# Attention and rational MLP on one core: quad 1's loads moved from the software queue to the two hardware issuers, products of zeros ahead of the first transposes, and a re-searched static plan

One core of a Trainium2 chip. The metric is device time of one execution in microseconds (us); most executions agree within 0.3%. "g1" is the product with w_in throughout, and "the start" is the time of its first matmul.

## The reference

```python
# ... cut: m is each row's maximum, h2 = h * h, h3 = h2 * h ...
scores = scale * np.matmul(q, k.transpose(0, 1, 3, 2))      # q, k, v: 8 x 12 x 448 x 64, float32
e = np.exp(scores - m)
attn = e / (np.sum(e, axis=-1, keepdims=True) + np.exp(-m) + 1e-09)
x = np.matmul(attn, v)      # then heads joined: 3584 x 768
h = x @ w_in                # 768 x 2048
P = a[0] + a[1] * h + a[2] * h2 + a[3] * h3
Q = 1.0 + np.abs(b[0]) * np.abs(h) + np.abs(b[1]) * h2
out = (P / (Q + 1e-06)) @ w_out                              # 2048 x 768
```

## The kernel before

Every instruction is an `Op` with an engine, an estimated duration and dependencies. A small simulation in the kernel file (`Plan`) merges several lists for each engine into one order, and the kernel emits that order. Changing a constant of the plan therefore reorders instructions without changing any of them.

Batch 0 is attended in half-width "units" (queries 0 to 223 of the four-head "quads" 0, 1, 2, ...), so that g1 can begin early. For quad 0, pieces of k and q come as float32 to staging tiles, are cast to float16, transposed on PE, copied from PSUM, multiplied to scores on PE and exponentiated on ScalarE:

```python
piece(0, 0, 0, 2, "ACT", 2.8, "ACT")     # k, pair 0, first half: issued by ACT, cast by ACT
piece(1, 0, 0, 2, "SP", 2.65, "DVE")     # q
piece(0, 0, 2, 2, "ACT", 3.4, "ACT")
piece(1, 1, 0, 2, "SP", 3.9, "DVE")
piece(0, 1, 0, 2, "ACT", 3.6, "ACT")
piece(0, 1, 2, 2, "SP", 3.7, "ACT")
for pr in range(2):
    piece(1, pr, 2, 2, "SP", 6.8, "DVE", True)      # late: waits for a stage
# ... cut ...
kload.append(load_op(1, k, kn, "k", kfree, NN))     # quad 1 by the software queue (POOL)
qload.append(load_op(1, q, qn, "q", qfree, NN))
loads(0, "v")
loads(2, "kq")
loads(1, "v")
loads(2, "v")
ORDER = "kq3 i kq4 i kq5 v3 i v4 i v5 o kq6 o o o"  # i, o: pieces of w_in, w_out
```

One unit's attention is 48 matmuls (16 for the sums of the exponentials, 32 with v), then a logarithm and an exponential on ScalarE that make the reciprocal:

```python
ln = Op(f"ln{i}", "ACT", 0.14 + 0.4 * f, [], None)
ex = Op(f"ex{i}", "ACT", 0.14 + 0.35 * f, [ln], None)
d = Op(f"a{i}d", "PE", 0.77 * f, [consts, hist(x_free, b, NX)] + e_ops[m0:m0 + 2 * npass],
       lambda: tiles(ud, lambda h, j: ones[0:P, :]), gen=(True, ud, ln), mode="a")
```

## Time and profile before

| | before |
|---|---|
| time, median of 3 | 432.91 us (432.63 to 433.24) |
| span of the profiled execution | 431.5 us |
| start (first g1 matmul) | 27.30 us |
| from the start to the end | 404.21 us, of it 1.35 us of PE stalls and 3.33 us after the last matmul |
| first exponential | 8.19 us |
| record of full TensorE clock begins | 18.08 us |

The time is the span and some 1.8 us around it. PE is close to solid behind the start, so a gain must come from an earlier start, from fewer stalls behind it, or from the tail. ScalarE paces the stretch ahead of it (15.49 us of work in the 19.18 from the first exponential on). In its order of time (columns: start, duration, instruction, and in brackets the idle time just before it with what ended it) the waits of the old stretch are:

```profile
10.22 1.92 ACT L480 ACTIVATE e<-sps 112x896 f16<-112x896 f32 x2 [0.32 <-PE sps L472]
12.78 1.72 ACT L480 ACTIVATE e<-sps 112x896 f16<-112x896 f32 x2 [0.64 <-PE sps L472]
14.92 0.45 ACT L521 ACTIVATE lden<-gen,one_c 128x224 f32<-128x224 f32 x1 [0.42 <-PE gen L507]
16.89 1.72 ACT L480 ACTIVATE e<-sps 112x896 f16<-112x896 f32 x2 [1.10 <-PE sps L472]
19.65 0.92 ACT L480 ACTIVATE e<-sps 112x896 f16<-112x896 f32 x1 [1.04 <-PE sps L472]
```

All of them end with a score pass or an attention group on PE: ScalarE waits for PE, and PE, at that time, runs slowly (16 attention matmuls take 0.94 us at 13.93 and 0.57 at 19.73) or waits for a load (k of quad 3, issued at 10.01 us, is waited for until 18.88).

### The profile page before, as it was taken

The numbers are of one execution on the slowest core, as the hardware profiler recorded it, in microseconds if no ns is written. First come the engines' busy times: TensorE is split into PE (matmuls) and PEld (weight loads), VectorE is DVE, ScalarE is ACT, GpSimd is POOL, SyncE is SP. The second block draws the span as 40 slices with busy tenths as digits, with TensorE's granted clock in tenths as the row PEclk, the third lists the DMA queues.
The fourth block names the chain that finished last, engine by engine and source line by source line (L and its number), as shares of the span: only waits on it lengthen the run. The fifth ranks groups of instructions, "written<-read, shape, count | busy, mean of one in ns | idle before, by whom it ended". The sixth has DMA issues, their size and how long they took to land.

```text
span 431.5 us, 8834 instructions
## 1 busy us (share of the span) xinstructions
PE 419.2 (97%) x3680; PEld 218.7 (51%) x3680; DVE 339.9 (79%) x505; ACT 327.8 (76%) x386; POOL 120.7 (28%) x172
## 2 busy tenths in 40 slices
PE   3999999999999999999999999999999999999996
PEld 2667665544444444444454444444444455555563
DVE  2445999998999887698998668979698788999800
ACT  4699999798888777888886897877798854578521
POOL 5655516566005340423703333052000000000000
PEclk9999999999999999999999999999999999999999
DMA  9999999899606947299399886373211011111132
GB/s 148 202 200 205 207 180 150 152 154 162 123 2 69 160 85 118 28 141 115 58 117 107 119 123 85 81 108 73 45 36 38 2 36 38 36 38 36 39 103 81
DMA packets 78153, 43.12 MB, mean 100 GB/s; under 512 B 36128, under 2 KB 74528, under 8 KB 78112
## 3 DMA queue, kind: packets, MB, share of 16 engines
q0 software_dynamic: 37856, 22.35, 39.7%
q1 hardware_dynamic: 39472, 19.80, 25.5%
q8 instruction: 29, 0.48, 0.5%
q10 hardware_dynamic: 784, 0.39, 0.4%
q14 instruction: 12, 0.10, 0.1%
HBM read 45.62 MB, written 11.01 MB: 131 GB/s over the span
## 4 chain that ended last, share of the span: by engine, by line
PE 89%; ACT 4%; DMA 3%; DVE 1%; issue 1%; ACTq 0%; POOLq 0%
PE gen L671 34%; PE gen L573 33%; PE gen L507 12%; PE sps L472 10%; DMA kn<-in_k_dram 2%; ACT e L480 2%; DMA h<-in_k_dram 1%; ACT c L625 1%; ACT c L628 1%; PE gen L389 1%; DVE h L590 0%; ACT lden L521 0%; DVE x L535 0%; ACT lden L523 0%; DVE c L614 0%
## 5 line engine op out<-in xcount | busy, mean ns | idle before, releaser
L480 ACT ACTIVATE e<-sps 112x896 f16<-112x896 f32 x192 | 167.1, 917 | 41.5 <-PE sps L472 41.1
L573 PE MATMUL gen<-x,w_in 128*128 128x448 f16 (+1 forms) x864 | 161.8, 332 | 0.0
L671 PE MATMUL gen<-w_out,g 128*128 128x384 f16 (+2 forms) x768 | 135.9, 326 | 0.0
L573 PEld LDWEIGHTS <-w_in 128*128 128x128 f16 x864 | 79.9, 98 | 68.3 <-issue 14.4
L671 PEld LDWEIGHTS <-g 128*128 128x128 f16 x768 | 72.7, 98 | 58.4 <-issue 10.4
L590 DVE CAST h<-gen 128x448 f16<-128x448 f32 x113 | 69.4, 618 | 24.4 <-PE gen L573 24.3
L614 DVE TENSOR_TENSOR n<-n,h 128x1792 f16<-128x1792 f16 x64 | 70.1, 1095 | 0.7
L625 ACT ACTIVATE c<-c,oneeps_c 128x1792 f16<-128x1792 f16 x32 | 57.3, 1791 | 11.4 <-DVE c L614 11.1
L472 PE MATMUL sps<-qt,kt 64*128 64x448 f16 (+1 forms) x432 | 58.4, 343 | 2.3 <-ACT e L480 1.1
L648 POOL COPY gx<-g 128x1024 f16<-128x1024 f16 x8 | 8.3, 1040 | 183.1 <-DVE g L614 183.1
L693 ACT ACTIVATE o<-gen 128x384 f32<-128x384 f32 (+2 forms) x56 | 27.4, 490 | 36.2 <-PE gen L671 36.0
L628 ACT ACTIVATE c<-c 128x1792 f16<-128x1792 f16 x32 | 54.6, 1705 | 0.3
L610 DVE TENSOR_SCALAR n<-n,abc 128x1792 f16<-128x1792 f16 x64 | 44.3, 693 | 1.1
L614 DVE TENSOR_TENSOR g<-n,c 128x1792 f16<-128x1792 f16 x32 | 35.1, 1098 | 12.8 <-ACT c L628 11.5
L433 POOL COPY kp<-kn 112x256 uint32<-112x256 uint32 x36 | 26.1, 755 | 57.2 <-DMA kt<-kp 50.3
L507 PE MATMUL gen<-e,vn 112*32 112x448 f16 (+1 forms) x864 | 41.8, 337 | 0.0
L535 DVE TENSOR_TENSOR x<-gen,lden 128x448 f16<-128x448 f32 (+1 forms) x54 | 28.3, 563 | 13.9 <-ACT lden L523 12.7
L614 DVE TENSOR_TENSOR c<-c,w 128x1792 f16<-128x1792 f16 x32 | 35.2, 1100 | 0.0
L472 PEld LDWEIGHTS <-kt 64*128 64x128 f16 x432 | 15.0, 96 | 36.5 <-issue 32.9
L507 PEld LDWEIGHTS <-vn 112*32 112x32 f16 x864 | 23.1, 99 | 14.0
L433 POOL COPY qp<-qn 112x256 uint32<-112x256 uint32 x36 | 25.2, 726 | 18.1 <-DMA qt<-qp 18.0
L610 DVE TENSOR_SCALAR n<-h,abc 128x1792 f16<-128x1792 f16 x32 | 24.7, 772 | 0.1
(42 smaller groups left out, 248.1 us busy)
## 6 DMA issues: line engine op xcount, KB each, us to landing
vn<-in_v_dram POOLq DMA_DIRECT2D x24, 224.0 KB, 8.5
kn<-in_k_dram POOLq DMA_DIRECT2D x23, 224.0 KB, 5.7
qn<-in_q_dram POOLq DMA_DIRECT2D x23, 224.0 KB, 7.4
w_in<-in_moe_w_in_dram POOLq DMA_DIRECT2D x12, 256.0 KB, 9.7
w_out<-in_moe_w_out_dram POOLq DMA_DIRECT2D x4, 768.0 KB, 16.2
out_dram<-o SPq DMA_DIRECT2D x8, 336.0 KB, 3.2
out_dram<-o SPq DMA_DIRECT2D x8, 288.0 KB, 2.8
out_dram<-o SPq DMA_DIRECT2D x7, 240.0 KB, 2.5
```

The costliest lines, as they stand in the source:

```text
L433: nc.gpsimd.tensor_copy(out=mid[0].bitcast(U32)[:, pr], in_=src[n % NN].bitcast(U32)[:, 2 * pr:2 * pr + 2] .rearrange("p e j d -> p j e d"))
L472: nc.tensor.matmul(out=sps[m % NS][0:(P if i == 0 and j == 1 else 128), hh, ci * qw:(ci + 1) * qw], lhsT=kt[n % NK][r, c0:c0 + (P if i == ...
L480: nc.scalar.activation(out=e_sb[m % NE], in_=sps[m % NS][0:P, :, 0:S], func=AF.Exp, scale=scale)
L507: nc.tensor.matmul(out=gen[unit["bank"]][32 * h:32 * h + 32, 0:qw], lhsT=lhs(h, j), rhs=e_sb[m % NE][:, h % 2, c0:c0 + qw], start=(j == 0) ...
L535: mult.emit = lambda s=s, uu=uu: nc.vector.tensor_tensor(out=x_sb[b % NX][:, 2 * qd + s, q0:q0 + qw], in0=gen[uu["bank"]][:, 0:qw], in1=ld ...
L573: nc.tensor.matmul(out=gen[unit["bank"]][:, fi * qw:(fi + 1) * qw], lhsT=w_in_sb[wg][:, c // 2, c % 2, (fc % FG) * 128:(fc % FG + 1) * 128 ...
L590: nc.vector.tensor_copy(out=dst, in_=src)
L610: return lambda: nc.vector.tensor_scalar(out=out, in0=in0, scalar1=s1, scalar2=s2, op0=op0, **kw)
L614: return lambda: nc.vector.tensor_tensor(out=out, in0=in0, in1=in1, op=ALU.mult)
L625: lambda: nc.scalar.activation(out=c, in_=c, func=AF.Ln, bias=oneeps_c)))
L628: lambda: nc.scalar.activation(out=c, in_=c, func=AF.Exp, scale=-1.0)))
L671: nc.tensor.matmul(out=gen[unit["bank"]][:, 0:wd], lhsT=lhs, rhs=w_out_sb[f][:, fc % FG, cols], start=(fc == 0), stop=(fc == NFC - 1))
```

## The change

The intent: let the clock of TensorE rise before the real work comes, by multiplying zeros while PE has nothing to do (that work raises it was the author's assumption; what the runs show of it stands below); give the pieces of quad 0 the DMA engines alone, and let quad 1 come by the two hardware issuers; and let the plan be searched again with a model of how loads share the DMA engines. The core of the diff:

```diff
+    def fill(n, out):
+        for _ in range(n):
+            nc.tensor.matmul(out=out[0:64, 0:P], lhsT=idle[0:P, 0:64], rhs=idle[0:P, :],
+                             start=True, stop=True)
+    FIRST = 32                    # zeros ahead of the first transposes
+    FILLS = (4, 4, 3, 1)          # ahead of score passes 0 to 3
     def scores ... emit:
+                    if m < len(FILLS):
+                        fill(FILLS[m], sps[m % NS][:, 0])
-        piece(0, 0, 0, 2, "ACT", 2.8, "ACT")
+        plan.add("c0", piece(0, 0, 0, 2, "ACT", 2.8))           # cast on DVE now
+        plan.add("c0", piece(0, 0, 2, 2, "ACT", 3.0, "ACT"))    # the one cast left to ACT
 ...
+            for ti, (src, dst, dma) in enumerate(((k, kn, "ACT"), (q, qn, "SP"))):
+                stage = quad1_stage(ti, pr)
+                d = load(dma, src, 4 + 2 * pr, 2, stage, 0, J, 4.3 + 1.1 * pr)
+                cast(1, ti, pr, 0, J, dst[1][:, 2 * pr:2 * pr + 2], stage, d)
 ...
-    kload.append(load_op(1, k, kn, "k", kfree, NN))
-    qload.append(load_op(1, q, qn, "q", qfree, NN))
+    vz = plan.add("cpt", Op("vz", "DVE", 0.06, [first_casts[0, 1, 0, 0]],
+                            lambda: nc.vector.memset(vn[0][:, 0, 0, 0:2], 0.0)))
     loads(0, "v")
+    vload[0].deps.append(vz)      # v of quad 0 held behind the first q cast
-    ORDER = "kq3 i kq4 i kq5 v3 i v4 i v5 o kq6 o o o"
+    ORDER = "kikiikivkkvoovoovkvv"
-    DUES = (0, 0, 4, 6)
-    LEAD = 45.0
+    DUES = (0, 0, 4.2, 3.0)
+    LEAD = 50.9
+    DUE = (28.1, 39.7, 51.4, 58.5, 76.4, ... cut ...)
-    TLEAD = 5.0
+    TLEAD = 4.6
-    LAG = {0: L0, 1: L1, B - 2: L6, B - 1: (8, 2)}
+    LAG = ((0, 3.5), (12.0, 1.8), (6.5, 2.4), (5.0, 1.9), (4.0, 3.4), (12.0, 1.8), (11.5, 2.8), (12.0, 1.3))
```

Cut: the new model of transfers, and bookkeeping that lets output tiles be planned in another order.

> **What bounds the kernel now.** I read the page first, then the busy time in stretches, the chain that ended last, the timelines of TensorE and ScalarE up to 30 us, and the DMA issues with their landings.
>
> ```profile
> PE 419.2 (97%) x3680; PEld 218.7 (51%) x3680; DVE 339.9 (79%) x505; ACT 327.8 (76%) x386; POOL 120.7 (28%) x172
> PE   3999999999999999999999999999999999999996
> DMA  9999999899606947299399886373211011111132
> ```
>
> TensorE is full from the second slice on. A busy PE is not a PE at its peak, so I split the trace at the first matmul of the first product with w_in (27.3 us; line L573, "g1" below):
>
> ```profile
> 0.00:8.19 8.19, 1.63 (x20) 1.01 (x20) 2.19 (x20) 2.74 (x5) 5.68 (x13) 1.00 0.76 135
> 8.19:27.37 19.18, 17.25 (x341) 11.46 (x340) 8.41 (x28) 15.49 (x23) 10.58 (x15) 1.00 1.36 200
> 27.37:67.30 39.93, 39.92 (x557) 26.99 (x558) 31.52 (x55) 37.88 (x47) 16.36 (x24) 1.00 1.30 197
> 67.30:399.58 332.28, 331.81 (x2595) 162.24 (x2592) 288.73 (x394) 262.40 (x299) 87.00 (x120) 1.00 0.58 84
> ```
>
> The first columns are stretch, length, PE busy. From 27.4 us PE has next to no idle time. There I took the gaps from matmul start to matmul start: g1 189 ns for 448 columns, the product with w_out 163 ns for 384, and each change of kind costs the same every time (0.19 us out of a score pass, 0.10 us into one from a product, 0.24 us out of an attention group). Gaps beyond these sum to about 1.3 us in 404 us. So behind g1 the kernel is a fixed amount of PE work, and only its start can be moved. Ahead of g1 the matmuls need about 11 to 13 us by those gaps, but 27.3 us pass: some 15 us are lost there, 4.0 of them before the first matmul.
>
> How they are lost, on ScalarE and PE:
>
> ```profile
> 7.56 0.72 ACT L351 ACTIVATE kn<-h 112x256 f16<-112x256 f32 x2 [2.74 <-DMA h<-in_k_dram]
> 8.19 1.70 ACT L480 ACTIVATE e<-sps 112x896 f16<-112x896 f32 x2
> ...
> 13.93 0.94 PE L507 MATMUL gen<-e,ones 112*32 112x224 f16 x16
> 17.15 0.59 PE L389 MATMUL gen<-ident,kn 112*64 112x112 f16 x8
> 18.93 0.39 PE L389 MATMUL gen<-ident,kn 112*64 112x112 f16 x8 [0.37 <-DMA kn<-in_k_dram]
> 19.73 0.57 PE L507 MATMUL gen<-e,ones 112*32 112x224 f16 x16
> ```
>
> ScalarE stands 2.74 us at a cast that waits for a piece of k; the first exponential, whose scores were ready at 5.5 us, starts at 8.19. And the same 16 matmuls take 0.94 us at 13.93 and 0.57 us at 19.73: PE runs cold. The trace's clock record for full speed begins at 18.08 us (the PEclk row does not show this). The chain says the rest:
>
> ```profile
> 1.72 5.82 DMA h<-in_k_dram
> 10.01 8.87 DMA kn<-in_k_dram
> ```
>
> Early pieces land late because the software queue was already filled behind them, and the k load of quad 3 is waited for at 18.88, ahead of unit 2's scores.
>
> [...]full speed is recorded from 18.08 to 431.10 us, which is 121.0 windows; the window 14.67 to 18.08 was full of work, the one before had a gap at 11.7 to 12.2. [...]a 112 KB piece issued at 0.74 us lands after 2.5 us, one issued at 8.00 into the backlog after 6.4.
>
> **The change part by part.**
>
> *Products of zeros.* 32 of 112 columns ahead of the first transposes, 4, 4, 3 and 1 ahead of the first score passes. [...] They need only a memset that ends near 0.9 us, so they run from about 1.1 to 4.1 us, in time in which PE idles (first transpose at 3.99). The cost is about 0.1 us there, and 12 x about 50 ns = 0.6 us later, most of it while PE waits for copies; I count 0.3 us. The gain: with the window grid of the trace (18.08 minus multiples of 3.413: 1.02, 4.43, 7.84) PE is warm at 4.4 or 7.8 us instead of 18.1. PE was busy without a gap from 12.2 to 18.1 us; at full clock (0.57 against 0.94, 0.39 against 0.59: ratio 0.6 to 0.66) these 5.9 us shrink to about 3.7.
>
> *First loads.* Quad 1's k and q come by four 224 KB loads (f32 in SBUF) on SP and ACT; the software queue starts with v of quad 0, held by a memset behind the first q cast (about 4.4 us). So the six first pieces have the DMA alone: at the 240 KB per us that the packets of 2 to 4 us show, 672 KB from 1.9 us are through at about 4.7 (before: 7.54), the 896 KB of quad 1 at about 8 (before: 8.87 and 10.08).
>
> *Casts.* Three of ScalarE's four k casts move to VectorE; the one left waits for a piece that landed at 4.38. The first exponential then starts behind its scores, about 5.4 us instead of 8.19: 2.8 us. VectorE gains three k casts and four casts of 512 columns, some 3 us, in a stretch in which it is busy 8.4 of 19.2 us; but they stand in front of copies and wait for landings, so the fourth exponential is held to about 9 us.
>
> *Order of loads.* Behind v0: k2, q2, v1, v2, k3, q3, w_in 0, k4, q4, w_in 1 and 2, k5, q5, w_in 3. One load of 224 KB lands per 1.15 us in a backlog, a w_in piece per 1.3. From about 9 us on: k2 10.5, q2 11.6, k3 15 to 16 (before 18.88), w_in 0 at 20 to 21 (before 23.45), w_in 3 near 36 (42.62). PE's order wants w_in 3 some 17 us behind g1: no wait.
>
> *The new plan behind g1.* In PE's order of both programs the matmuls behind g1 are the same (864 and 896 of the two products, 1152 of attention, 364 of scores) but 16 more transposes (0.4 us). Changes into and out of score passes are 102 and 102 before, 101 and 101 after. With the measured costs: 393.3 us before, 393.0 after. So 0.3 us gained.
>
> **The sum.** When does g1 start? ScalarE decides: until the reciprocal of unit 2 it has 14 exponentials at 0.80 us (start to start) and three pairs of 0.34 and 0.28: 13.1 us. Before, it took 17.95 us from 8.19 to 26.14, so 4.9 us were waits, and g1 came 1.2 us later. After: 5.4 + 13.1 + 1.2 = 19.7 us with no wait. A warm PE and earlier k3 take part of the 4.9; the held fourth exponential and quad 2's landing keep some. I choose 3 us: g1 at 22.7, 4.6 us earlier. With 0.3 of the plan gained, 0.3 for the zeros inside and 0.3 for new stalls: 432.9 - 4.6 - 0.3 + 0.3 + 0.3 = 428.6; the chance that some of the old 1.3 us of stalls goes brings me to 428.3.
>
> **Rivals.**
> 1. *The zeros don't warm it*, or the window grid falls otherwise and the sparse work after 4 us doesn't hold it. The cold loss stays in part; the loads and casts alone give about 2.5 us: 430.4. For it: 4 to 12 us had some half of the time in work and stayed cold. Against: the three runs agree to 0.6 us.
> 2. *ScalarE becomes the bound later.* The new plan draws attention forward: unit 16 starts 141 us behind g1 instead of 160. Summing start-to-start times in ScalarE's order, work up to unit 16's last exponential exceeds PE's position there by 5.4 us; at units 3 to 5 it is 13.8 in both programs, so 8 us of slack are left against the start. VectorE: 3.7 at unit 15 against 14.5 at unit 0. But waits between the engines in the denser plan could cost 1 to 3 us: 430 to 431.
> 3. *DMA only moves the wait.* The engines are full until about 50 us; the f32 staging writes twice the bytes of a cast load. If quad 2 lands 2 us later than I say, g1 starts near 24.5: 430.2.
> 4. *Everything fits*: g1 near 20 us, 425.6.
>
> **Range and chances.** 2% is 8.7 us; even g1 at its floor of 19.7 and all old stalls gone give 7.6 + 1.3 + 0.3 = 9.2 us, so faster by over 2% needs everything at once. Slower by over 2% needs over 13 us of new stalls behind g1, which neither engine's sums show. Eight in ten: 425.6 (rival 4) to 431.0 (rivals 1 and 2 in part).
>
> **What would show it.** Clock record at full from 4.4 or 7.8 us; 16 attention matmuls at 0.57 us from the first group on; first exponential at 5.3 to 5.7 us, no long ScalarE wait at a cast; first matmul with w_in at 22 to 23.5 us; PE idle behind it under 2 us and score changes as counted. Wrong if PE stays cold beyond 8 us, if g1 comes at 25 us or later, or if g1 is early but PE waits for ScalarE or VectorE between 100 and 170 us.

Where cuts are marked, statements about the hardware that no trace of this case shows are taken out, among them the working-out of the zeros' length (3.0 us), from which "about 1.1 to 4.1 us" comes. The changed kernel's trace has the 32 zeros from 0.98 us to the first transpose at 3.98, so 94 ns each; at full clock ten of them took 0.48 us (8.03 to 8.51, second profile with zeros in the waits). No term of the sum itself is cut: it came to 428.6 us, and to 428.3 with fewer stalls. But its 3 us of waits rest on a PE that is warm at 4.4 or 7.8 us, and that on the author's assumption that a "window" of 3.413 us full of work raises the clock. The grid of these windows is borne out by the records below, the assumption only in part.

## The result

The changed kernel took 431.74 us (median of 430.96, 431.62, 431.92, 431.85), the kernel before 432.77 (432.91, 432.63, 433.24, 432.04). All runs are in the fast state. Ratio 0.9974, 95% interval 0.9955 to 0.9993; in a later call with more rounds 0.9965 (0.9950 to 0.9981). Ratios here are the mean time of one kernel's fast runs over that of the other's in the same rounds, so not quite the ratio of the medians. The change gains 1 to 1.5 us where 4.6 were predicted: "within 2%" holds, the range 425.6 to 431.0 doesn't.

From the changed kernel's page, the shares of the engines and the row of TensorE's clock (before, that row shows 9 in all 40 slices):

```profile
PE 421.0 (98%) x3724; PEld 222.1 (52%) x3724; DVE 340.1 (79%) x514; ACT 328.1 (76%) x383; POOL 112.3 (26%) x170
PEclk8799999999999999999999999999999999999999
```

The 44 more matmuls are the zeros. A changed kernel that looks colder than the one before is an artefact: the record of before begins only at 18.08 us, with the full clock, and its row shows 9 ahead of that too, although 16 attention matmuls take 0.94 us there (at 13.93), as long as in the changed kernel at a recorded clock of 0.50 (at 12.44). The changed kernel's record reads: full from 4.88 to 8.30 us, half to 15.12, full to 428.14. These stretches are 1, 2 and 121 times 3.413 us long, and the full one of before 121 times; a window, below, is one such 3.41 us, counted from the steps of its profile. **The clock rose as early as predicted and fell again one window later.** Busy time by these windows (columns: stretch, length, PE busy and matmuls, granted clock, DMA share, GB/s; the 1.00 ahead of the first step, at 4.88 us, is the same artefact, as the zeros there take 94 ns each):

```profile
1.47:4.88 3.41, 3.41 (x42) 1.00 0.80 212
4.88:8.30 3.42, 2.29 (x36) 1.00 1.08 264
8.30:11.71 3.41, 2.65 (x33) 0.50 1.44 197
11.71:15.12 3.41, 3.41 (x68) 0.50 1.41 202
```

The zeros and the first eight transposes fill the first window entirely. In the next one PE has 2.29 us of work in 3.42, and behind it the clock is at 0.50. ScalarE in the changed kernel, in its order of time:

```profile
5.59 0.90 ACT L540 ACTIVATE e<-sps 112x896 f16<-112x896 f32 x1
6.81 0.92 ACT L540 ACTIVATE e<-sps 112x896 f16<-112x896 f32 x1 [0.32 <-PE sps L532]
7.94 0.92 ACT L540 ACTIVATE e<-sps 112x896 f16<-112x896 f32 x1 [0.22 <-PE sps L532]
10.09 2.53 ACT L540 ACTIVATE e<-sps 112x896 f16<-112x896 f32 x3 [1.23 <-PE sps L532]
13.43 0.45 ACT L581 ACTIVATE lden<-gen,one_c 128x224 f32<-128x224 f32 x1 [0.80 <-PE gen L567]
15.35 2.58 ACT L540 ACTIVATE e<-sps 112x896 f16<-112x896 f32 x3 [1.05 <-PE sps L532]
```

The first exponential comes at 5.59 us instead of 8.19: that gain is there. Then the waits: 1.23, 0.80 and 1.05 us are the large ones. I count waits as the prediction did, from the first exponential to the first one behind unit 2's reciprocal, less 13.1 us of work: 4.7 us before (8.19 to 26.03; the prediction's 4.9 took 26.14 from the chain) and 4.9 after (5.59 to 23.58). None of it has gone. What stands behind the last two waits is PE at half clock (0.50 by the record; at full clock the same 16 and 32 matmuls take 0.57 and 0.94 us, fourth profile below), as its order of time shows:

```profile
12.44 0.94 PE L567 MATMUL gen<-e,ones 112*32 112x224 f16 x16
13.16 1.71 PE L567 MATMUL gen<-e,vn 112*32 112x224 f16 x32
```

and what stands behind the 1.23 us is a load. The chain of waits (start, duration, what) goes from the landing of quad 1's k to the score pass that unit 0 waits for, though that pass uses no data of quad 1: the cast and the transposes of quad 1 stand ahead of it in the orders of VectorE and PE.

```profile
2.23 5.56 DMA g<-in_k_dram
...
7.81 0.67 DVE kn L375
...
8.52 0.96 PE gen L446 x16
...
9.56 0.51 PE sps L532 x4
...
10.09 0.93 ACT e L540
```

So the start comes at 24.85 us, 2.45 earlier than in the first profile of before. Behind it, 404.31 us against 404.21: PE stalls 1.00 against 1.35 us (gaps from matmul start to matmul start beyond what the same change of kind costs elsewhere), but 3.75 against 3.33 us after the last matmul.

### The profile page after: what moved, and what is told of

Read it like the earlier page. It is cut to its first block, busy times and chain, and to the rows that moved or that the text cites. A ratio compares the mean times of both kernels' runs of the same rounds, so it can differ in the third digit from the quotient of the medians.

```text
span 429.2 us, 8939 instructions
## 1 busy us (share of the span) xinstructions
PE 421.0 (98%) x3724; PEld 222.1 (52%) x3724; DVE 340.1 (79%) x514; ACT 328.1 (76%) x383; POOL 112.3 (26%) x170
## 4 chain that ended last, share of the span: by engine, by line
PE 90%; DVE 5%; ACT 2%; DMA 1%; ACTq 0%; issue 0%
PE gen L731 35%; PE gen L633 33%; PE gen L567 12%; PE sps L532 10%; ACT e L540 2%; DMA g<-in_k_dram 1%; DVE n L670 1%; DVE n L674 1%; DVE h L650 1%; DVE c L674 0%; PE gen L446 0%; DVE c L670 0%; ACTq L370 0%; DVE qt L454 0%; DVE kt L454 0%; DVE w L670 0%
## 5 line engine op out<-in xcount | busy, mean ns | idle before, releaser
L532 PE MATMUL sps<-qt,kt 64*128 64x448 f16 (+1 forms) x432 | 57.3, 338 | 2.0 <-ACT e L540 1.3
L708 POOL COPY gx<-g 128x1024 f16<-128x1024 f16 x8 | 9.4, 1173 | 155.0 <-DVE g L674 155.0
L491 POOL COPY kp<-kn 112x256 uint32<-112x256 uint32 x36 | 23.0, 667 | 42.7 <-DMA kt<-kp 38.8
L329 POOL DMA_DIRECT2D vn<-in_v_dram x24 | 17.5, 732 | 57.5 <-PE sps L532 43.9
```

The lines of the kernel that those rows point to most:

```text
L532: nc.tensor.matmul(out=sps[m % NS][0:(P if i == 0 and j == 1 else 128), hh, ci * qw:(ci + 1) * qw], lhsT=kt[n % NK][r, c0:c0 + (P if i == ...
```

## Experiments

Sixteen runs, all correct. Single looks (the last four) have state "unknown"; every other one has its profile from an execution in the fast state, and of all their executions one is slow (438.12 us, with both orders and the zeros).

### Are the zeros worth anything by themselves?

Without zeros:

```diff
-    FIRST = 32
-    FILLS = (4, 4, 3, 1)
+    FIRST = 0
+    FILLS = (0, 0, 0, 0)
```

> The changed kernel without its 44 products of zeros, all else equal. Theory A (the zeros warm TensorE for one window only, 4.9 to 8.3 us, and the clock drops again to 15.1 us because too little work follows): without them the clock record starts at 11.7 to 18.1 us, once, and stays; the first matmul with w_in comes 0.3 to 1.0 us later than the changed kernel's 24.85, so about 0.5 us slower than the changed kernel, 1.5 to 2 us faster than the kernel before in the profiled span. Rival B (the clock at the start is not on the path, loads and casts decide): within 0.2 us of the changed kernel. Rival C (the zeros cost more than they give): 0.3 us or more faster than the changed kernel.

431.39 us, 0.9968 (0.9953 to 0.9984): the same as with them. The profiled execution has its first exponential at 5.63, full clock from 15.27 us only, and the start at 25.10. The kernel before with the 44 zeros:

```diff
+        nc.vector.memset(idle, 0.0)
+    FIRST = 32
+    FILLS = (4, 4, 3, 1)      # and the two calls of fill() as in the change
```

> The kernel before with the same 44 products of zeros and nothing else. Theory A: warm for one window at most, then cold again, since the kernel before has still less work between 4.4 and 7.8 us (it waits for the pieces of k until 7.5): 0 to 0.7 us faster than the kernel before. Rival B: 0. Rival D (a clock that is held makes the dense stretch 12.2 to 18.1 us shorter by 2.2 us): 2 us faster, which needs the clock at full from 8 us on.

432.85 us, 1.0003 (0.9983 to 1.0023); in its profile the clock is full from 17.51 us and the start is at 27.44. Products of zeros in this number are neutral in either kernel. The early first exponential is the work of loads and casts alone.

### Can the clock be held, and what is that worth?

84 more zeros, ahead of score passes and transposes up to pass 11:

```diff
-    FILLS = (4, 4, 3, 1)
+    FILLS = (4, 8, 8, 2, 6, 6, 8, 8, 4, 4, 4, 4)
+    TFILLS = {2: 6, 4: 4, 8: 12, 10: 8}       # zeros ahead of these transposes
```

> The changed kernel with 84 more products of zeros, spread over the first 12 score passes and four groups of transposes, most where TensorE waits[...]. Theory A (the clock's drop at 8.30 us and the cold stretch to 15.12 us cost about 2 us): the clock record has no gap after its first start, the 16 attention matmuls of unit 0 take 0.57 us and not 0.94, first matmul with w_in at 22.7 to 23.5 us, total 1.3 to 2.0 us below the changed kernel. Rival B (ScalarE waits for landings and for VectorE's casts, whatever the clock): clock held, but the first matmul with w_in stays at 24.5 to 25, same time within 0.3 us. Rival C: the zeros stand in TensorE's order ahead of what is wanted, and eat the gain.

432.13 us, 0.9984 (0.9969 to 0.9999). The clock is full from 6.93 us without a gap, yet the start is at 25.84. The chain says why (shares of the chain up to 27 us): the zeros themselves are its largest part.

```profile
by line: PE sps L272 26.0%; PE sps L536 17.2%; PE gen L450 12.5%; PE gen L571 10.1%; ACT e L544 9.5%; PE gen L272 7.3%; issue 4.9%; PE gen L637 2.5%; DVE x L599 2.2%; ACT lden L585 1.6%; DVE kt L458 1.5%; ACT lden L587 1.0%; DVE qt L458 0.7
```

So I put 29 more zeros only where PE had been waiting:

```diff
-    FILLS = (4, 4, 3, 1)
+    FILLS = (4, 4, 4, 1)
+    TFILLS = {2: 4, 4: 4, 8: 12}
+    PRE = {5: (10, 8)}                         # 8 ahead of score pass 5
```

> The changed kernel with 29 more products of zeros, put only where TensorE waits in its trace: 4 ahead of the transposes at 5.7 and 6.7 us, 12 ahead of quad 1's (7.9 to 8.5 us), 8 into a free bank ahead of score pass 5 (10.5 to 11.0), one more ahead of pass 2. Theory A' (a held clock is worth some 1.5 us, which the zeros on TensorE's path ate in the run with 84 more): clock at full without a gap from its first start, exponential 6 at 13.8 to 14.3 us and not 15.35, first w_in matmul at 23.5 to 24, 1 us faster than the changed kernel. Rival E (the clock moves ScalarE's waits only from one place to another, because landings of k and q follow): first w_in matmul 24.5 to 25.5, same time as without any zeros (431.4) within 0.4 us.

430.48 us, 0.9958 (0.9941 to 0.9976). In the profile the clock is full from 10.72 us; the start is at 24.48. Repeated beside the changed kernel on one chip:

> The changed kernel with 29 more products of zeros where TensorE waits, once more, now beside the changed kernel on the same chip. If holding the clock is worth about 1 us without the zeros standing on the path, ratio 0.995 to 0.996 to the kernel before and 0.5 to 1.2 us under the changed kernel. If the ratio of 0.9958 was the luck of its chip, it comes out at 0.997 to 0.998, level with the changed kernel. In the profile: full clock from before 11 us without a gap, attention group of unit 0 at about 1.0 us of matmul spacing instead of 2.3.

430.27 us, 0.9954 (0.9934 to 0.9974), against 431.18 us, 0.9965 (0.9950 to 0.9981), of the changed kernel. It is the best version that I ran and beats the kernel before by 0.4 to 0.5%; against the changed kernel the intervals overlap, so that part (0.9 us of medians) isn't established. In this profile the clock is full from 4.38 us and stays, and the start is at 23.35.

### Is it the order of quad 1's work?

No zeros, and quad 1's casts and transposes behind unit 0's last score pass:

```diff
-            more = {-1: first[:2], 0: first[2:3], 1: first[3:], 2: nxt[:2]}
+            more = {-1: first[:2], 0: first[2:3], 1: first[3:], 3: nxt[:2]}
```

> No zeros; quad 1's casts on VectorE and transposes on TensorE put behind what unit 0's last score pass needs. Theory F (the fourth exponential waits 1.3 to 1.9 us for quad 1's landing and casts though it uses no data of quad 1): exponential 3 at 9.2 us or earlier instead of 10.1 to 10.5, and the first w_in matmul 0.3 to 0.8 us earlier than in the run without zeros (25.10), as the fifth exponential still needs quad 1. Rival E: the wait only moves to exponential 4, nothing gained.

430.85 us, 0.9965 (0.9949 to 0.9980), no better than without zeros alone. The fourth exponential comes at 9.43 instead of 10.47, the fifth, which does need quad 1, at 10.92 and the seventh at 14.90. The start (26.84) can't be compared here, as the plan put one more attention group ahead of it. With unit 0's attention moved behind unit 1's third score pass as well:

```diff
-            if t == 1:
+            if t == (2 if i == 1 else 1):
```

> As the run before it, and unit 0's attention group (48 matmuls, 2.4 us on a cold TensorE) behind unit 1's third score pass. Theory G (ScalarE's longest wait, between exponentials 5 and 6, is TensorE's order: score pass 6 stands behind the cold attention group): exponential 6 at 13.2 to 13.8 us, first w_in matmul 1 to 1.5 us earlier than without zeros. Rival: the reciprocal of unit 0 comes later by what is gained, and the end stays.

433.26 us, 1.0024 (1.0004 to 1.0044). The seventh exponential comes at 13.27, the eighth then only at 16.13: the wait moved by one pass. And both together with the zeros in the waits:

> Both changes of order, and the zeros in the waits. Theory A' with F and G: the effects add in part: first w_in matmul at 22.5 to 23.5 us, 1.5 to 2 us faster than the changed kernel, 429.7 to 430.2. Rival E: 431 or more.

432.51 us, 1.0014 (0.9978 to 1.0050; two of six executions are far out: 436.74, which counts as fast and is in the ratio, and 438.12, which is slow and is not; no run explains them). Here the clock is full from 5.15 us and the start is at 24.03, but 406.76 us follow it, 2.66 of them stalls. The two other orders of quad 1's work gain no time. They pass waits on, within the stretch or to what comes behind the start.

### The plan or the start?

The changed kernel with the plan's old constants:

```diff
-    DUES = (0, 0, 4.2, 3.0)
+    DUES = (0, 0, 4, 6)          # LEAD, due times, TLEAD and LAG of before too
```

> The changed kernel with the due times, lead and lags of the kernel before (the search's results behind the first w_in matmul undone; loads, casts and zeros kept). If the new plan behind that matmul is neutral, as the two traces say (404.2 us behind it before, 404.3 after): same time as the changed kernel within 0.5 us. If the old constants don't fit the earlier start: new waits of TensorE behind it, 0.5 to 2 us slower than the changed kernel.

432.32 us, 0.9996 (0.9979 to 1.0013), start at 25.89. The other half, the new constants on the first loads and casts of before, without zeros:

```diff
-        plan.add("c0", piece(0, 0, 0, 2, "ACT", 2.8))
+        piece(0, 0, 0, 2, "ACT", 2.8, "ACT")      # and so on: loads and casts of before
```

> The first loads and casts of the kernel before, no zeros, but the changed constants of the plan. If the plan is what gains, ratio 0.997 to 0.998, with g1 at 27 us and the stretch behind it at 403 to 404 us. If the earlier first pieces and the plan are only worth something together (the old plan on the new start gave 0.9996), ratio 1.000, with g1 at 26 to 27.5 us and 404.3 us or more behind it. A plan that was searched for another start may also lose: then 1.001 to 1.004.

432.96 us, 1.0007 (0.9986 to 1.0028), start at 26.36. Neither half gains anything measurable; together they gain 0.3%. (The interval of the old plan and that of the changed kernel, 0.9950 to 0.9981, overlap slightly, so what the new plan adds to the new loads isn't established.) This run also dates the tail: 3.33 us after the last matmul, as before, while the old plan on the new loads has 3.75. The longer tail goes with the loads: in all profiles it is 3.33 to 3.43 us with the loads of before and 3.60 to 3.77 with the new ones.

### How far do two profiles of one kernel differ?

> The kernel before, unchanged, as a kernel of its own: shows how far two sets of runs of the same instructions differ, and gives a second profile. All theories expect a ratio of 1.000 with an interval of at most 0.002 to each side. Should it miss 1 by 0.002 or more, differences of that size among the other runs (0.9968 without zeros, 0.9958 with zeros in the waits) tell nothing. In its profile g1 at 27.1 to 27.5 us, 404.2 to 404.6 us behind it, and the clock's full step first seen between 15 and 18.5 us.

Ratio 1.0002 (0.9988 to 1.0017), as expected of the same instructions. But its profile has the start at 25.98, not 27.1 to 27.5, and 405.18 us behind it with 2.23 us of stalls: the page that the prediction rests on shows a late start of this kernel. Its clock was full from 14.87 us instead of 18.08.

> The changed kernel, unchanged: the common reference of this call, and a second profile. Expected ratio 0.997 (0.9974 in the first result), span 429.2 to 430.2. My theory says that the early full clock comes and goes again, because the second window has too little work: full by about 5 to 7 us, half again before 12 us, full for good at 14 to 18 us. The rival, that the drop in the first profile was a chance of the phase, expects a clock that stays full from 5 us in this one.

Here both theories missed. The clock never rose early: it is full from 16.38 us on. The zeros, 0.98 to 4.1 us, fell on both sides of a boundary at 2.73 us (counted back from that step), and the windows behind it had 3.17, 3.17 and 2.87 us of work; the clock was full only behind the next, with 3.41. Every execution lists its mean granted clock, and this says how often the other case comes, as cold time ahead of the first step doesn't count there (1.000 in the first profile of before, full from 18.08 us) and a clock that is lost again does: 0.988 to 0.992 in six of the changed kernel's twelve executions (the first profile, with two windows lost, has 0.991), and never below 0.998 without zeros or in the kernel before. A rise with a drop behind it is thus common, and it is worth nothing that shows: in this call the three executions at 0.991 have a mean of 430.96 us, the other three 431.56, and the ranges (430.51 to 431.38, 430.93 to 432.26) overlap.

(The 0.37 in the third of the next expectations stands in no view: that window was 67% busy, 2.29 us of 3.42.) What was left open was whether the clock or the landings set the start. Four more looks, two of each version:

> The version with 29 more zeros in the waits, only for a third profile of it. Its two profiles have the clock full from 10.72 us with the first w_in matmul at 24.48, and full from 4.38 us with it at 23.35: 0.18 us per us of half clock. If the clock sets the start, this profile lies within 0.35 us of 23.35 + 0.18 x (start of full clock - 4.38), with ScalarE's waits growing in step. If that was chance, the start has nothing to do with the clock record.

> The same once more: within 0.35 us of 23.35 + 0.18 x (start of full clock - 4.38), if the clock sets the start.

> The changed kernel for a third profile. Its two have half clock for 7.3 us and for 12.0 us behind 4.4 us, with the first w_in matmul at 24.85 and 25.46: 0.13 us per us. If the clock sets the start, this one lies within 0.35 us of 24.85 + 0.13 x (half clock behind 4.4 us - 7.3). A clock that comes early and stays would put it at 23.9 and would speak against my reading that the second window always has too little work (0.37).

> The same once more: within 0.35 us of 24.85 + 0.13 x (half clock behind 4.4 us - 7.3).

All profiles of the three kernels, in us ("waits": ScalarE's, counted as above):

| kernel | clock full | first exp. | waits | start | stalls behind it | after last matmul | span |
|---|---|---|---|---|---|---|---|
| before, 1 | from 18.08 | 8.19 | 4.7 | 27.30 | 1.35 | 3.33 | 431.5 |
| before, 2 | from 14.87 | 7.69 | 3.7 | 25.98 | 2.23 | 3.41 | 431.2 |
| changed, 1 | 4.88 to 8.30, from 15.12 | 5.59 | 4.9 | 24.85 | 1.00 | 3.75 | 429.2 |
| changed, 2 | from 16.38 | 5.72 | 5.4 | 25.46 | 0.84 | 3.77 | 429.7 |
| changed, 3 | 10.43 to 20.67, from 24.08 | 5.86 | 4.6 | 24.92 | 1.20 | 3.63 | 429.3 |
| changed, 4 | from 10.73 | 5.82 | 3.4 | 23.57 | 0.85 | 3.63 | 427.6 |
| zeros in waits, 1 | from 10.72 | 5.51 | 4.6 | 24.48 | 1.92 | 3.73 | 429.7 |
| zeros in waits, 2 | from 4.38 | 5.59 | 3.4 | 23.35 | 1.26 | 3.61 | 427.8 |
| zeros in waits, 3 | from 5.12 | 5.69 | 3.8 | 23.86 | 2.64 | 3.76 | 429.9 |
| zeros in waits, 4 | from 6.32 | 5.63 | 3.6 | 23.60 | 1.81 | 3.68 | 428.7 |

My lines through two points each failed in part: for the changed kernel's fourth profile they gave 24.7, and it started at 23.57; for the zeros in the waits, third profile, 23.5 against 23.86, just outside; the other two hit (24.92 against 25.13, 23.60 against 23.70). It isn't the number of cold microseconds that counts but which ones. What separates 23.6 from 24.9 to 25.5 in the changed kernel is whether the clock is full and stays full from about 10.7 us, when the first attention group and the 32 transposes around it stand on ScalarE's path. PE and ScalarE in the fourth profile of the changed kernel, to be held against the same lines of the first:

```profile
12.19 0.57 PE L567 MATMUL gen<-e,ones 112*32 112x224 f16 x16
12.59 0.94 PE L567 MATMUL gen<-e,vn 112*32 112x224 f16 x32
```

```profile
10.41 2.53 ACT L540 ACTIVATE e<-sps 112x896 f16<-112x896 f32 x3 [0.70 <-PE sps L532]
12.82 0.46 ACT L581 ACTIVATE lden<-gen,one_c 128x224 f32<-128x224 f32 x1
...
13.87 2.58 ACT L540 ACTIVATE e<-sps 112x896 f16<-112x896 f32 x3 [0.17 <-PE sps L532]
```

The waits of 0.80 and 1.05 us have shrunk to nothing and 0.17. From the fourth exponential to the seventh it is 3.46 us here and 5.26 in the first profile. Ten profiles have this stretch in the same order (added zeros aside), and they fall into two groups: 3.45 to 3.50 us in the six whose clock is full there, or in all but its first 0.3 us (changed 3 and 4, all four with zeros in the waits), 5.14 to 5.31 in the four whose clock is half (changed 1 and 2, without zeros, old plan). So the half clock costs some 1.8 us in this stretch. The run with 84 more zeros shows the other side: full clock and still 4.74 us, as its zeros stand in between. The landings are not the reason: in the fourth profile quad 1's k came at 8.33 and 10.05 us and quad 2's at 12.03, in the first at 7.78, 9.65 and 11.74, so all were later in the faster one, and k of quad 3 came at 17.57 and 17.59. It is the same kernel, and it took 429.36 us in that execution.

The third profile shows how landing and clock are tied. There k of quad 3 landed at 18.43 us, 0.9 later, and PE waited; the window around it lost the clock, which then cost the attention group behind it 2.35 us instead of 1.26, and the start went from where the fourth has it to 24.92. PE's order of time, and the windows (busy of PE, PEld, DVE, ACT and POOL with their counts, then clock, DMA share and GB/s):

```profile
18.48 0.39 PE L446 MATMUL gen<-ident,kn 112*64 112x112 f16 x8 [0.95 <-DMA kn<-in_k_dram]
```

```profile
13.84:17.26 3.42, 3.07 (x94) 2.33 (x92) 2.06 (x7) 3.30 (x5) 1.21 (x2) 1.00 1.38 207
17.26:20.67 3.41, 2.35 (x44) 1.28 (x46) 1.96 (x8) 2.64 (x5) 2.12 (x3) 1.00 1.27 206
20.67:24.08 3.41, 3.41 (x64) 2.29 (x64) 0.00 (x0) 2.83 (x5) 1.49 (x3) 0.50 1.37 198
```

The windows of the version with zeros in the waits, second profile, show what the added zeros do in the stretch in which the changed kernel's first profile had 2.29:

```profile
0.96:4.38 3.42, 3.40 (x41) 3.38 (x42) 0.85 (x18) 0.41 (x1) 0.29 (x1) 1.00 0.72 204
4.38:7.79 3.41, 2.75 (x50) 2.00 (x48) 1.95 (x8) 3.01 (x4) 3.34 (x5) 1.00 1.04 258
```

2.75 us of work held the clock. But its first profile, with other boundaries, had a window without idle time that didn't raise it (3.90 to 7.31; the next one did):

```profile
3.90:7.31 3.41, 3.41 (x40) 2.40 (x39) 1.62 (x8) 2.68 (x4) 2.98 (x5) 1.00 1.00 258
7.31:10.72 3.41, 3.41 (x51) 2.98 (x48) 1.32 (x6) 1.67 (x2) 2.60 (x4) 1.00 1.34 198
```

So here the clock was held with less work than stood ahead of any rise, and PE's busy time alone doesn't tell whether it rises. In the windows that I read out for eight of the profiles (both of before, the four of the changed kernel, the first two of this version) the full clock was kept through all with 2.75 to 3.07 us of work and lost behind the two with less, 2.29 and 2.35. It rose behind windows with 3.33 to 3.41 us of work and behind none with 3.17 or less, but the one above with 3.41 didn't raise it.

Profile 1 of this version also shows what such zeros cost at half clock. It had the full clock from 10.72 us, as the fourth profile of the changed kernel had from 10.73, and quad 1's k landed earlier (8.01 and 9.65 against 8.33 and 10.05), yet its fourth exponential comes at 11.34 against 10.41 and its start at 24.48 against 23.57. At half clock the score pass ahead starts at 8.48 instead of 8.20 us, and 12 zeros then stand before the transposes of quad 1, which start at 9.81 instead of 8.84:

```profile
8.96 1.14 PE L272 MATMUL gen<-idle 112*64 112x112 f16 x10
11.34 2.53 ACT L549 ACTIVATE e<-sps 112x896 f16<-112x896 f32 x3 [1.35 <-PE sps L541]
```

In three of this version's four profiles part of the start is given back: in profiles 1, 3 and 4 a score pass near 65 us waits 0.7 to 1.3 us for a transpose by DMA, which no profile of the changed kernel has.

## Why the prediction was wrong

**The failed step** is "A warm PE and earlier k3 take part of the 4.9 ... I choose 3 us: g1 at 22.7". It rests on the step "PE is warm at 4.4 or 7.8 us instead of 18.1", taken over from the phase of one profile, and on the silent assumption that a warm clock stays. What the runs showed instead, by terms of its sum:

- *Clock.* Zeros from "about 1.1 to 4.1 us" is right (3.19 us, from 0.98). But 3 us of zeros fill a 3.41 us window only at some phases: of the changed kernel's four profiles one rose at once and dropped after a single window, one rose at 16.38, two near 10.5, long after the first zeros. By the granted clocks seven of its twelve executions (0.996 or less) had the full clock and lost it again, so the assumption that a warm clock stays failed in more than half of them. Where the clock was half, the stretch from the fourth to the seventh exponential took some 1.8 us longer. The prediction used the grid of one profile as if it were fixed; counted back from the steps, boundaries of the changed kernel fall at 1.47, 2.73, 0.19 and 0.50 us in its four profiles.
- *Waits.* 4.9, 5.4, 4.6 and 3.4 us instead of 3.0. With the full clock from 10.7 us on, 3.4 is what is left, so the choice of 3 was within 0.4 us for the case that the prediction described; the start then came at 23.57, and 23.35 with the clock from 4.38 us (zeros in the waits), inside its "22 to 23.5 us" or just beside. That this is the rare case was the mistake.
- *First exponential.* 5.4 predicted, 5.59 to 5.86 measured; right, and worth 2.2 us between the means of the two and the four profiles.
- *Loads.* The first pieces "through at about 4.7": the last two landed at 5.87 and 6.24, and they did not have "the DMA alone", as quad 1's loads were issued from 2.17 us on. Quad 1 "at about 8": 7.5 to 9.65. k of quads 2 and 3 at "10.5" and "15 to 16": 11.74 and 17.59. "w_in 0 at 20 to 21": its last piece at 22.67 to 23.70, no earlier than in the two profiles of before (23.45 and 22.40). So the loads run 1.2 to about 3 us late from the first pieces on. It counts where PE waits for k of quad 3 (third profile), and w_in left a start at 22.7 next to no room.
- *Fourth exponential* "held to about 9 us": 10.09. Undoing that order (the quad 1 experiment) brought it to 9.43 and left the time alone.
- *Fixed work behind the start*, "393.3 us before, 393.0 after": the stretch behind it less stalls and tail is 399.5 and 399.6, so that 0.3 isn't there. (The level of the sum is 6 us short of that stretch, in both kernels; I did not trace why.)
- *Stalls.* "0.3 for new stalls", and part of the old 1.3 may go: 0.84 to 1.20 against 1.35 and 2.23. Better than predicted.
- *Tail.* Not in the sum: 0.3 us more on average (3.63 to 3.77 against 3.33 and 3.41), with the loads.

The difference for the first pair of profiles: the span changed by 2.35 us instead of 4.6. Of these 2.25, the start explains 2.15 (24.85 against 22.7), the fixed work 0.3, the tail 0.4; the stalls and the allowance of 0.3 for zeros give 0.65 back. The rest up to 431.74 is the choice of profiles: the one of before was 433.28, 0.4 above its median, that of the changed kernel 0.8 below.

**The rivals.** The first one ("the window grid falls otherwise or the sparse work after 4 us doesn't hold it") named what happened, and should have had most of the chance; its 430.4 is still 1.3 us short of the result. The second (ScalarE bounds later) isn't seen: PE is busy for all of the 70 us between 100 and 170 us in all four profiles. That its "430 to 431" ended nearer is luck. The third (DMA only moves the wait) shows in part, as the 1.23 us behind quad 1's landing. The argument against the first, that three runs agree to 0.6 us, was void: a clock that rises late in every run of the kernel before says nothing about the phase, and even its own start differs by 1.3 us between two profiles while the spans, 431.5 and 431.2, are nearly alike.

What stays open: what decides whether a window raises the clock; why the longer tail comes with the loads (after the last landing SyncE has 5 or 6 closing semaphore waits instead of 2, which take 0.32 to 0.39 us instead of 0.14, but no run isolates that); and whether the version with zeros in the waits really beats the changed kernel.

## What to carry to other kernels

Before counting on an early full clock, ask two questions of every window (3.41 us here) at every phase: is it filled, and does the next one hold it? In this case it rose behind 3.33 to 3.41 us of work, held with 2.75 and more, and was lost behind 2.35 and 2.29. The zeros here, shorter than two windows, depended on the phase (3.19 us of them filled a window in one of four profiles), and the 84 that stood in the engine's order cost what they gained (start at 25.84 us, with the full clock from 6.93). Those placed in known waits stayed in them only where the clock was full: at half clock ten of them took 0.85 us (8.96 to 9.81) instead of 0.48 (8.03 to 8.51), and that profile lost 0.9 us of its start. And one profile of a kernel whose phase varies is a sample: the start of the same instructions moved by 1.3 us here, so take two or three before a prediction of a few microseconds rests on it.
